# A Sinkhorn sort with a matrix column on each partition and row sums by fp32 matmul, and a stored order for every engine, in a fused attention and gating kernel

**Chip, cores, metric.** One core of a Trainium2 chip. The metric is device microseconds (us) of one execution, median over runs. Lower is better.

## The reference, cut to what matters

```python
P = sort_net                                   # (4, 8, 8, 8): 32 matrices of 8x8
for _ in range(5):
    P = exp(P - max(P, axis=-1))
    P = P / (sum(P, axis=-1) + 1e-9)           # rows
    P = P / (sum(P, axis=-2) + 1e-9)           # columns
k_sorted = einsum('bhij,bhjcd->bhicd', P, k_b) # 8 blocks of 96 rows are mixed
v_sorted = einsum('bhij,bhjcd->bhicd', P, v_b)
# attention inside each block of 96 rows, then x @ w_in, a scan over the
# 768 rows, silu gating, and @ w_out
```

The five iterations are tiny (2,048 numbers) but strictly serial, and nothing that needs sorted K or V can start before them.

## The kernel before

The program is a list of operations with dependences. A planner in the kernel orders them on the five engines when the program is built; what runs on the chip are five fixed lists, one for each engine, each run in order. The sort puts one 8x8 matrix on each of 32 partitions and takes seven steps an iteration, one on ScalarE (ACT) and six on VectorE (DVE):

```python
for it in range(5):
    op("sk_exp", ACT,  exp(E8, src))                     # 32x64
    op("sk_rs",  DVE,  tensor_reduce(RS, E9, add))       # row sums
    op("sk_rr",  DVE,  reciprocal(RS))
    op("sk_pa",  DVE,  tensor_tensor(PA8, E8, rs, mult))
    op("sk_cs",  DVE,  tensor_reduce(CS, PA9t, add))     # column sums
    op("sk_cr",  DVE,  reciprocal(CS))
    op("sk_pb",  DVE,  tensor_tensor(dst, PA8, cs, mult))
# ... cut: transpose on TensorE, copy, 8 small matmuls spread P over 128 partitions
op("lmat0", DVE, LALL = spread P * MASK)                 # block matrices of heads 0, 1
# warm-ups: matmuls with nothing to do, 48 in all
WARMS = (3, 3, 2, 2, 1)                                  # groups of 4 (last: 8)
# ... cut
op("vs%d_%d", PE, matmul(PS, LALL[head], VB[head]))      # sorted V of one head
op("vse%d_%d", ACT or DVE, copy to VSS)
op("vm%d", SP, 8 DMAs VA <- VSS)                         # "V move": re-lays a batch's V
P.schedule(8, pull=5.859375, stick=0.1, nudge=NUDGE)
```

(Schematic; names are the program's.) Sorted V of batches 1 to 3 needs eight value products, eight evictions to VSS and then the V move before its attention can begin.

The softmax here doesn't subtract the row's maximum and nothing guards it: scores larger than these inputs give would overflow.

## Time and profile before

| | kernel before |
|---|---|
| time | 123.95 us median of 3 runs (123.77 to 125.11) |
| profiled span | 121.7 us |
| TensorE (PE) busy | 92% of the span |
| LALL, the first sorted block matrices | starts at 12.26 us |
| a 128x128 matmul on PE takes 314 ns until, and 219 ns from | about 10.6 us |
| first V move leaves at | 28.55 us |

PE is the bound once sorted data are there (busy 103.75 of the 105.86 us from 12.74 to 118.6). Groups of the same matmuls in the timeline (columns: start us, us from the first start to the last end, engine, line, operation, operands, count, idle time before):

```profile
5.04 0.85 PE L609 MATMUL PSA<-IDENT,QB 128*64 128x128 bf16 x12 [0.92 <-DMA QB<-in_q_dram]
...
12.15 0.53 PE L609 MATMUL PSA<-IDENT,QB 128*64 128x128 bf16 x12
```

Twelve transposes of Q take 0.85 us at 5 us and 0.53 us at 12 us. I call PE *cold* and *warm* for these two rates; the warm-ups are meant to get from one to the other before LALL. The granted clock of the profile does not show the difference: it gives 1.00 for the first 12 us, but the trace's first clock record is at 10.86 us.

### The profile page before, as it was taken

To read this page: it belongs to the slowest core of one execution; us is meant where nothing else is said; L and a number is where in the kernel's file an instruction comes from. 1 tells how busy PE (TensorE), PEld (TensorE's weight loads), DVE (VectorE), ACT (ScalarE), POOL (GpSimd) and SP (SyncE) were. 2 spreads that over 40 slices of the span, in tenths; PEclk is the share of its full clock that TensorE was granted. 3 is DMA by queue.
4 is the path that set the end of the run, shared out by engine and by line. 5 is a ranking of instruction groups with operands and counts; after the bars stand their busy time and mean duration, and the time that the engine had idled before them with its cause. 6 is when DMAs were issued, how large, how long until landed. Compare 5 with 4: busy or idle time off the path is not lost.

```text
span 121.7 us, 3684 instructions
## 1 busy us (share of the span) xinstructions
PE 112.2 (92%) x1485; PEld 74.7 (61%) x1485; DVE 100.0 (82%) x239; ACT 84.0 (69%) x183; POOL 59.5 (49%) x84
## 2 busy tenths in 40 slices
PE   1689989999999999999999999999799999999990
PEld 1577778765766777667556586766466655554530
DVE  3774897999998999977599999999799999995300
ACT  4126879999868988898866977887634423365761
POOL 7999999999955620200028065000011396235500
PEclk9999999999999999999999999999999999999999
DMA  1999999999999999999999868289892000422665
GB/s 6 149 176 188 199 212 209 204 205 203 217 247 236 202 208 215 225 251 239 253 293 251 128 102 154 100 151 144 287 260 48 5 0 0 172 89 86 226 252 216
DMA packets 26305, 21.33 MB, mean 175 GB/s; under 512 B 7472, under 2 KB 22832, under 8 KB 26288
## 3 DMA queue, kind: packets, MB, share of 16 engines
q0 software_dynamic: 13824, 11.01, 58.3%
q1 hardware_dynamic: 12464, 10.08, 30.8%
q8 instruction: 12, 0.20, 0.6%
q14 instruction: 5, 0.04, 0.1%
HBM read 22.03 MB, written 6.29 MB: 233 GB/s over the span
## 4 chain that ended last, share of the span: by engine, by line
PE 66%; DMA 10%; DVE 9%; ACT 4%; SPq 4%; POOL 2%; issue 1%; POOLq 0%
PE PSA L800 31%; PE PSA L836 14%; DMA VA<-VSS 6%; PE PSA L733 5%; DVE XN L754 5%; DMA QB<-in_q_dram 4%; SPq L671 4%; PE PSA L703 4%; PE PSA L609 4%; PE PSA L625 3%; PE PSA L662 2%; ACT EX L713 2%; PE PSA L776 1%; DVE XT L417 1%; DVE RZ L745 1%
## 5 line engine op out<-in xcount | busy, mean ns | idle before, releaser
L819 POOL TENSOR_TENSOR GA<-GA,YS 128x384 bf16<-128x384 bf16 x30 | 27.2, 917 | 55.3 <-DVE GA L816 32.0
L800 PE MATMUL PSA<-XT,WIN 128*128 128x384 bf16 x256 | 45.4, 326 | 0.8 <-DVE XN L754 0.8
L800 PEld LDWEIGHTS PSA<-XT,WIN 128*128 128x128 bf16 x256 | 23.9, 98 | 16.3 <-DVE XN L754 0.9
L713 ACT ACTIVATE EX<-PSA 96x384 bf16<-96x384 f32 x64 | 26.3, 488 | 2.4 <-PE PSA L703 2.1
L813 ACT ACTIVATE TH<-PSA 128x384 f32<-128x384 f32 x32 | 15.7, 492 | 15.0 <-PE PSA L800 13.8
L836 PE MATMUL PSA<-WOUT,GA 128*128 128x512 bf16 (+1 forms) x100 | 23.2, 370 | 0.0
L754 DVE TENSOR_TENSOR XN<-PSA,RZ 96x320 bf16<-96x320 f32 (+2 forms) x49 | 21.7, 470 | 0.2
L816 DVE SCALAR_TENSOR_TENSOR GA<-TH,PSA 128x384 bf16<-128x384 f32 x32 | 17.0, 542 | 5.3 <-ACT TH L813 4.2
L415 ACT ACTIVATE OUTSB<-PSA 128x512 f32<-128x512 f32 (+1 forms) x23 | 13.4, 581 | 7.3 <-PE PSA L836 7.1
L807 DVE TENSOR_TENSOR_SCAN YS<-AEXP,YS,PSA 128x384 bf16<-128x384 f32 x16 | 15.7, 999 | 0.3 <-PE PSA L800 0.2
L807 DVE TENSOR_TENSOR_SCAN YS<-AEXP,PSA 128x384 bf16<-128x384 f32 x16 | 14.8, 940 | 0.7 <-PE PSA L800 0.7
L733 PE MATMUL PSA<-VA,EX 96*128 96x65 bf16 x256 | 13.7, 194 | 0.5 <-DVE XN L754 0.2
L836 PEld LDWEIGHTS PSA<-WOUT,GA 128*128 128x128 bf16 x100 | 9.0, 97 | 8.2 <-ACT OUTSB L415 0.3
L733 PEld LDWEIGHTS PSA<-VA,EX 96*128 96x128 bf16 x256 | 10.9, 98 | 4.7 <-DMA VA<-VSS 0.8
L745 DVE RECIPROCAL RZ<-PSA 96x5 f32<-96x5 f32 (+2 forms) x52 | 8.3, 175 | 2.0 <-PE PSA L733 1.6
L415 ACT ACTIVATE KTS<-PSA 128x768 bf16<-128x768 f32 x11 | 8.6, 811 | 1.4 <-PE PSA L625 1.3
L703 PE MATMUL PSA<-QTS,KTS 64*96 64x96 bf16 x256 | 9.5, 210 | 0.0
L703 PEld LDWEIGHTS PSA<-QTS,KTS 64*96 64x96 bf16 x256 | 7.2, 121 | 3.6 <-DVE KTS L417 0.4
L609 PE MATMUL PSA<-IDENT,QB 128*64 128x128 bf16 x192 | 7.8, 238 | 1.3 <-DMA QB<-in_q_dram 1.3
L415 ACT ACTIVATE VSS<-PSA 128x384 bf16<-128x384 f32 x19 | 8.4, 504 | 0.3 <-PE PSA L662 0.3
L625 PE MATMUL PSA<-LALL,KB 128*64 128x128 bf16 x192 | 7.4, 221 | 0.7 <-ACT EX L713 0.6
L427 POOL DMA_DIRECT2D QB<-in_q_dram x10 | 7.7, 782 | 0.3 <-issue 0.3
(60 smaller groups left out, 122.2 us busy)
## 6 DMA issues: line engine op xcount, KB each, us to landing
out_dram<-OUTSB SPq DMA_DIRECT2D x23, 256.0 KB, 2.5
VA<-VSS SPq DMA_DIRECT2D x24, 97.5 KB, 5.7
VB<-in_v_dram POOLq DMA_DIRECT2D x6, 384.0 KB, 20.1
KB<-in_k_dram POOLq DMA_DIRECT2D x6, 384.0 KB, 23.9
QB<-in_q_dram POOLq DMA_DIRECT2D x6, 384.0 KB, 21.5
WIN<-in_moe_w_in_dram POOLq DMA_DIRECT2D x1, 1024.0 KB, 11.1
QB<-in_q_dram POOLq DMA_DIRECT2D x4, 192.0 KB, 5.1
KB<-in_k_dram POOLq DMA_DIRECT2D x4, 192.0 KB, 6.1
```

The lines of the kernel that those rows point to most:

```text
L415: return eng.activation(dst, src, AF.Copy, scale=1.0 if scale is None else scale)
L609: ins = e.transpose(PSB[u.bank][64 * x:64 * x + 64, t * 128:(t + 1) * 128], QB[sl][:, 2 * pr + x, t * 64:(t + 1) * 64], IDENT[:, :])
L703: ins = e.matmul(PS[us[half, x].bank][0:BLK, il * BLK:(il + 1) * BLK], KTS[ks][r, i * BLK:(i + 1) * BLK], qt(r, i))
L713: op("ex%d_%d_%d" % (p, half, x), act_cost(HALF), lambda e, n, u=us[half, x], es=es, half=half: e.activation(EX[es][:, half, 0:HALF].rearr ...
L733: ins = e.matmul(PS[u.bank][:, (kk - k0) * 65:(kk - k0 + 1) * 65], EX[es][:, i // 4, (i % 4) * BLK:(i % 4) * BLK + 128], VA[vs][:, i, hx * ...
L754: return e.tensor_tensor(XN[xs][:, k0 * D:(k0 + nb) * D].rearrange("p (n d) -> p n d", d=D), pv(u, nb)[:, :, 0:64], bass.AP(RZ[rz], 0, [[6 ...
L800: ins = e.matmul(PS[u.bank][:, 0:HALF], WIN[:, c, col:col + 128], XT[(4 * b + c) % NXT][:, half * HALF:(half + 1) * HALF], start=(c == 0), ...
L807: op("sc%d_%d_%d" % (b, ch, half), {"DVE": 65 + 384 * 2.1}, lambda e, n, u=u: e.tensor_tensor_scan(YS[slot][:, :], AEXP[:, ch:ch + 1].to_b ...
L813: op("th%d_%d_%d" % (b, ch, half), act_cost(HALF), lambda e, n, u=w: e.activation(TH[ts][:, :], PS[u.bank][:, 0:HALF], AF.Tanh, scale=0.5) ...
L816: op("ga%d_%d_%d" % (b, ch, half), dve_cost(HALF), lambda e, n, u=w: e.scalar_tensor_tensor(GA[slot][:, :], TH[ts][:, :], 1.0, PS[u.bank][ ...
L819: op("um%d_%d_%d" % (b, ch, half), {"POOL": 900, "DVE": 500} if b == B - 1 and half else {"POOL": 900}, lambda e, n: e.tensor_tensor(GA[sl ...
L836: ins = e.matmul(PS[u.bank][:, 0:c1 - c0], GA[slots[ch]][:, tl * 128:(tl + 1) * 128], WOUT[:, ch, c0:c1], start=(ch == 0), stop=(ch == 3))
```

## The change

Intent: shorten the serial chain. A column of a matrix now lies on each partition (256 partitions in two halves of 128, which run interleaved). Sums over a matrix row then cross partitions and become an fp32 matmul with blocks of ones; column sums fall out of a multiply as its accumulated output; the column scaling is folded into the next exp as its per-partition scale. Four dependent steps and a matmul replace seven steps, and the ending is shorter. At the same time the planner's rule is replaced by a stored list for each engine.

```diff
-ORDER is worked out:  P.schedule(8, pull=5.859375, stick=0.1, nudge=NUDGE)
+ORDER is stored:      P.replay(8, ORDER)
-WARM = 7500.0        # planner: PE is warm from here, ns
+WARM = 6000.0
-WARMS = (3, 3, 2, 2, 1)          # 48 warm-up matmuls
+WARMS = (4, 2, 2, 2, 2, 2)       # 14 groups of 3
-op("ld_sort", SP, dma PIN <- sort_net)
+for x in range(2):
+    o1 = op("ld_sort%d" % x, SP, dma SX[x] <- 128 rows of 8)
+    if x: o1.deps[ld_s] = 1       # the second waits for the first
+  # first iteration: exp(SM <- SX, accum_out=SR), reciprocal, block product SB,
+  #   scaled copy SA, fp32 matmul SB x SA, reciprocal           (cut)
+  for it in range(1, 5):
+    op("sk_exp%d_%d", ACT, activation(SE, SA or PSUM, Exp, scale=SC))
+    op("sk_mm%d_%d",  PE,  matmul(acc, BO, SE))          # fp32, 128x8: row sums
+    op("sk_rr%d_%d",  DVE, reciprocal(rrow, acc))
+    op("sk_pa%d_%d",  DVE, scalar_tensor_tensor(SA, SE, 1.0, rrow, mult, mult, accum_out=SR))
+    op("sk_cr%d_%d",  DVE, reciprocal(SC, SR))
+  # one matmul per half in place of transpose, copy and 8 matmuls (cut)
```

All the rest of the program is the same work in another order.

## The prediction

> **What bounds the kernel now.** I read the page first, then the chain that ended last in order of time, then the table of stretches, then the timeline of the first 24 us. The page says that TensorE (PE) is the engine to look at:
>
> ```profile
> span 121.7 us, 3684 instructions
> PE 112.2 (92%) x1485; PEld 74.7 (61%) x1485; DVE 100.0 (82%) x239; ACT 84.0 (69%) x183; POOL 59.5 (49%) x84
> PE 66%; DMA 10%; DVE 9%; ACT 4%; SPq 4%; POOL 2%; issue 1%; POOLq 0%
> ```
>
> PE is busy for 92% of the span and carries 66% of the chain. The measured time, 123.95 us, is about 2.2 us longer than the profiled span. The table of stretches, cut where the first matmul on sorted data starts (12.74 us) and where PE ends (118.6 us), has columns busy us of PE, PEld, DVE, ACT, POOL, then granted clock, DMA share and GB/s:
>
> ```profile
> 12.74:15.00 2.26, 2.10 (x58) 1.69 (x60) 2.01 (x3) 2.26 (x4) 2.26 (x9) 1.00 1.31 201
> 15.00:18.00 3.00, 2.41 (x61) 2.05 (x57) 2.86 (x4) 2.57 (x7) 3.00 (x6) 1.00 1.22 213
> 18.00:24.00 6.00, 5.93 (x137) 4.97 (x132) 5.24 (x21) 5.64 (x12) 5.97 (x8) 1.00 1.20 206
> 24.00:60.00 36.00, 35.73 (x549) 24.15 (x549) 31.57 (x75) 31.79 (x76) 16.58 (x21) 1.00 1.27 224
> 60.00:118.60 58.60, 57.58 (x593) 34.74 (x590) 50.71 (x104) 36.31 (x77) 19.84 (x22) 1.00 0.61 146
> ```
>
> In these 105.86 us PE is busy 103.75: only 2.1 us of idle time are left. So the time is (start of sorted work, 12.74) + (about 104 us of PE work) + (2 us of idle) + (tail of 3.1 us after PE's end: one eviction of 0.60 and a store of 2.5). The sort iteration can change the first term only. The timeline shows it as a chain of single small instructions, one after the other on ScalarE (ACT) and VectorE (DVE):
>
> ```profile
> 1.09 1.28 ACT L517 ACT_TABLE_LOAD   x1 [1.09 <-DVE PSA L492]
> 2.39 0.22 ACT L517 ACTIVATE PSA<-PIN 32x64 f32<-32x64 f32 x1
> ...
> 4.09 0.22 ACT L517 ACTIVATE PSA<-PBT 32x64 f32<-32x64 f32 x1 [1.49 <-DVE PBT L529]
> 4.34 0.22 DVE L520 TENSOR_REDUCE RS<-PSA 32x8 f32<-32x72 f32 x1 [0.28 <-ACT PSA L517]
> 4.60 0.19 DVE L522 RECIPROCAL RS<-RS 32x8 f32<-32x8 f32 x1
> ...
> 11.38 0.20 PE L545 MATMUL PSA<-IDENT,PBF 32*64 32x32 bf16 x1
> 11.62 0.18 DVE L548 CAST PT<-PSA 64x32 bf16<-64x32 f32 x1 [0.73 <-PE PSA L545]
> ...
> 12.26 1.42 DVE L560 TENSOR_TENSOR LALL<-PSA,MASK 128x256 bf16<-128x256 f32 x2 [0.46 <-PE PSA L554]
> ```
>
> The reader is to see three things. Exp to exp is 4.09 - 2.39 = 1.70 us: seven steps of about 0.243 us. The table load was over (2.37) just as the input landed (0.75 + 1.6 = 2.35), so it cost nothing. And after the fifth iteration a transpose, a copy and eight matmuls stand before LALL, the block matrices, at 12.26.
>
> [...]
>
> **The change part by part.** The 256 matrix rows go to two halves of 128 partitions, which run interleaved.
>
> Start. The first exp now also needs a constant that GpSimd (POOL) writes, and in POOL's new list that memset stands behind iota, the first Q load and another memset. In the trace POOL's first load is issued from 1.35 to 2.24, so the constant is there at about 2.4. In the old program the table load waited for the memsets of DVE (1.09, just after the second one ended at 1.01) and the exp alone for the DMA; I expect the same of the new one. Then the table load runs from about 2.45 to 3.75, and the first exp starts at 3.75 in place of 2.39: **+1.35 us** on the path.
>
> First iteration: [...]reciprocal 0.2; [...]reciprocal 0.2. About 1.9 us, so the second exp is at 5.65.
>
> Iterations two to five: [...]matmul to the next DVE instruction: 0.24 is what the bf16 one at 11.38 took[...]; reciprocal 0.22; [...]reciprocal 0.19. Sum 1.51 against 1.70. The other half's three DVE operations fit between, since independent DVE operations follow each other at less than their duration (two 96x4 reciprocals took 0.24 together). I take 1.55. The fifth exp is at 5.65 + 3 x 1.55 = 10.3.
>
> End: [...]reciprocal, multiply, mask reduction beside it, reciprocal: 1.0, masked product 128x128 0.3, matmul 0.25. LALL starts at 10.3 + 2.4 = **12.7 against 12.26**. So the shorter iteration (4 x 0.15 = 0.6) and the shorter ending (three steps gone, about 0.5) are eaten by the late table load. Without that the start would be 11.4.
>
> After LALL. I counted PE's new list: the order of all work is new. Changes of tile mode go from 55 to 59[...], seven groups of three warm-up matmuls come after LALL's matmul[...], and both first evictions (V and K) are on ACT one after the other, where before one was on DVE beside it; the first attention exp may come 1 us later than 15.16. The last seven output pieces are alike, so the tail stays. Against this: the order is a stored list, not the outcome of a rule, and I suppose that it was chosen because it was short; it can win at most the 2.1 us of idle time[...]. I put -1.3 there. Sum: +0.4 (start) + 0.4 (head and modes) - 1.3 = -0.5, so **123.4 us**.
>
> **The rivals.** (a) The sort path really becomes shorter: if the table load is hidden as before, or fp32 matmuls take 0.4, LALL comes at 10.8 to 11.4 and all of PE's work moves forward by about 1 to 1.5; with a better order 121.3. For it: the design aims at this. Against: the old trace puts the table load behind the memset wait, and K and V data limit it: the fourth to twelfth loads land about 1 us apart, from 8.95 to 17.6 (10.35 + 7.3), whatever the sort does, and the first K load is now the seventh, about 11.7. (b) The lockstep of two halves is slow: DVE, ACT and PE each run in order, so each half waits for the other; with 1.75 per iteration and a PE clock that warms late, LALL comes at 13.6 and the time is 125. For it: the old PE needed until about 10.6 to warm with 48 dense warm-ups, the new ones are sparser. (c) The start is hidden anyway and only the new order counts: POOL now has products of the gating before some loads, so late loads could make PE wait at 40 to 70 us; or the order closes PE's idle time. 122 to 125.
>
> **Range and chances.** (a) has some 25%, (b) 25%, the middle the rest. 2% is 2.5 us; faster than 121.5 needs both an earlier start and a better order: 14%. Slower than 126.4 needs (b) and a worse order: 6%. Range 121.2 to 125.4; the old runs alone spread from 123.77 to 125.11.
>
> **What would show it.** In the new profile: the table load starting after 2.3 and the first exp near 3.7 (if at 2.4, rival a); exp to exp 1.5 to 1.6 for one half (1.75 or more, rival b); matmul to reciprocal 0.5 to 0.6; LALL at 12.0 to 13.4; PE's idle time from there to its end 1 to 2.5 us. I am wrong if LALL starts before 11.5 or PE's work after it, idle included, differs by over 2 us from 105.9.

The sums were made with the cut terms. The first iteration's 1.9 us is 0.4 for the two reciprocals and 1.5 of cut terms. The 1.51 of an iteration is 0.41 for its two reciprocals (0.22 and 0.19 are durations of DVE steps in the profile above) and 1.10 of cut terms for exp, matmul and multiply (the 0.24 that still stands beside the matmul is a measured time and not the term); the range for "matmul to reciprocal" rests on them too. The 2.4 of the ending is 1.55 for the steps that still stand and about 0.85 of cut terms. The 1.55 is an estimate from the trace of the kernel before: 0.19 + 0.22 + 0.38 + 0.19 for the four small steps, about 0.3 for 128 columns from the 0.43 and 0.96 us that masked products of 256 and 768 columns took, and 0.24 for the matmul. The "0.4 (head and modes)" was for four more changes of tile mode; that a change costs time was not shown. With all of this the forecast came to +0.4 + 0.4 - 1.3 = -0.5, so 123.4 us. (One 96x4 reciprocal alone took 0.17 us, beside the 0.24 for two.)

## The result and the profile after

| | before | after |
|---|---|---|
| time, median | 123.86 us (123.75 to 125.11, 4 runs) | **135.69 us** (135.12 to 137.80, 4 runs) |
| ratio of fast runs | 1 | 1.0915 (95%: 1.0815 to 1.1015) |
| profiled span, clock | 121.7 us, 1.00 | 133.2 us, 0.974 |

A ratio here and below is the mean time of one kernel's fast runs over the mean of the other's fast runs of the same rounds, so it is not quite the ratio of the medians that stand beside it. A run is called slow when it lies over 1.5% above the fastest run of its kernel; the others are fast.

The page of the changed kernel:

```profile
span 133.2 us, 3729 instructions
...
PE 120.4 (90%) x1496; PEld 80.9 (61%) x1496; DVE 98.1 (74%) x251; ACT 87.3 (66%) x201; POOL 58.8 (44%) x90
...
PEclk9999999999999995599999999999999999999999
```

PE is busy 120.4 us in place of 112.2 for the same real work, and the clock row (tenths, 40 slices) falls to half near 52 us. So some of PE's time went into running slowly and some into waiting. The first 16 us, ACT and the first LALL on DVE:

```profile
2.51 1.28 ACT L494 ACT_TABLE_LOAD   x1 [2.51 <-POOL SX L488]
3.80 0.21 ACT L494 ACTIVATE SM<-SX 128x9 f32<-128x9 f32 x1
3.92 0.19 ACT L494 ACTIVATION_READ_ACCUMULATOR SM<-SX 128x1 f32 x1
...
5.32 0.21 ACT L494 ACTIVATE SM<-SX 128x9 f32<-128x9 f32 x1 [0.68 <-PE PSA L508]
...
5.53 0.26 ACT L519 ACTIVATE SE<-PSA,SC 128x8 f32<-128x8 f32 x1
...
7.47 0.29 ACT L519 ACTIVATE SE<-SA,SC 128x8 f32<-128x8 f32 x1
9.00 0.65 ACT L519 ACTIVATE SE<-SA,SC 128x8 f32<-128x8 f32 x2 [1.24 <-DVE SC L532]
11.30 0.65 ACT L519 ACTIVATE SE<-SA,SC 128x8 f32<-128x8 f32 x2 [1.66 <-DVE SC L532]
...
15.37 0.42 DVE L556 TENSOR_TENSOR LALL<-PSA,MASK 128x256 bf16<-128x256 f32 x1
```

The first half's exps are at 5.53 and 7.47: 1.94 us apart. The pairs at 9.00 and 11.30 hold both halves, 2.3 apart. The old exps were 1.70 apart. LALL comes 3.1 us later than before. On PE:

```profile
16.49 0.85 PE L630 MATMUL PSA<-LALL,KB 128*64 128x128 bf16 x12
...
46.25 0.81 PE L805 MATMUL PSA<-XT,WIN 128*128 128x384 bf16 x4
46.90 0.33 PE L667 MATMUL PSA<-VB,LALL 128*128 128x384 bf16 x1
50.60 0.49 PE L738 MATMUL PSA<-VA,EX 96*128 96x65 bf16 x6 [3.38 <-DMA VA<-VSS]
...
51.85 1.49 PE L805 MATMUL PSA<-XT,WIN 128*128 128x384 bf16 x4
```

Three things are to be seen. At 16.49 PE is still cold (0.85 for twelve, 0.53 before), although its list has been without a gap from 4.69 to 15.65; it turns warm near 18.9, against 10.6. After the matmul of 46.90 it stops for 3.38 us, from 47.22 on, for a V move. Behind that stop four projections take 1.49 us instead of 0.81. The same stretch in the table by stretches (busy us of PE, PEld, DVE, ACT, POOL; granted clock; DMA share; GB/s):

```profile
48.00:52.00 4.00, 1.40 (x10) 0.92 (x11) 1.44 (x3) 0.55 (x2) 0.00 (x0) 0.71 1.30 212
52.00:56.00 4.00, 4.00 (x23) 2.15 (x22) 2.28 (x7) 2.18 (x6) 1.72 (x2) 0.50 1.29 199
```

In the kernel before:

```profile
48.00:52.00 4.00, 4.00 (x65) 2.65 (x63) 3.76 (x9) 3.37 (x8) 0.91 (x1) 1.00 1.28 235
52.00:56.00 4.00, 4.00 (x86) 3.00 (x84) 3.10 (x9) 3.51 (x8) 0.00 (x0) 1.00 1.21 250
```

It has 65 and 86 matmuls in these two windows, at clock 1.00. Now there are 10 and 23. The trace's own clock records say the same: half clock is granted from 49.71 us, 2.5 us into the stop, for 6.83 us. At a granted clock of 0.50 that is up to 3.4 us of PE work lost (an estimate, half of 6.83), as much as the stop itself. The V move was late mainly because it left late. From the queue of the DMA issues, before and then after:

```profile
28.55 5.22 SPq L671 DMA_DIRECT2D VA<-VSS  x8
```

```profile
37.06 30.53 SPq L676 DMA_DIRECT2D VA<-VSS  x16
```

(The second line joins two moves: the first leaves at 37.06.) Its last piece landed at 50.5, against 40.3 before: 8.5 of these 10.2 us are the later start. It left late because the last value evictions of that batch stand on ACT behind 20 small normalisations (XN) and two activations of the gating (TH), with ACT busy 11.98 of the 12 us from 24 to 36 us:

```profile
34.14 1.76 ACT L756 ACTIVATE XN<-PSA,RZ 96x64 bf16<-96x64 f32 x8
35.72 0.56 ACT L818 ACTIVATE TH<-PSA 128x384 f32<-128x384 f32 x1
36.09 0.94 ACT L373 ACTIVATE VSS<-PSA 128x384 bf16<-128x384 f32 x2
```

So there were two suspects: the new sort, with its cold PE, and the stored order. All runs below gave a result that agrees with the reference, those with rounding to bf16 included.

### The profile page after: what moved, and what is told of

The parts are those of the page before. It is cut to its first block, busy times and chain, and to the rows that moved or that the text cites. A ratio compares the mean times of both kernels' runs of the same rounds, so it can differ in the third digit from the quotient of the medians.

```text
span 133.2 us, 3729 instructions
## 1 busy us (share of the span) xinstructions
PE 120.4 (90%) x1496; PEld 80.9 (61%) x1496; DVE 98.1 (74%) x251; ACT 87.3 (66%) x201; POOL 58.8 (44%) x90
## 4 chain that ended last, share of the span: by engine, by line
PE 66%; ACT 13%; DMA 9%; SPq 7%; issue 1%; POOL 1%; DVE 1%; POOLq 0%; ACTq 0%
PE PSA L805 27%; PE PSA L841 14%; DMA VA<-VSS 9%; SPq L676 7%; PE PSA L738 4%; PE PSA L630 4%; ACT EX L718 4%; PE PSA L708 3%; PE PSA L548 3%; PE PSA L614 3%; ACT XN L756 3%; PE PSA L524 2%; ACT VSS L373 2%; PE PSA L667 2%; PE PSA L652 1%
## 5 line engine op out<-in xcount | busy, mean ns | idle before, releaser
L805 PE MATMUL PSA<-XT,WIN 128*128 128x384 bf16 x256 | 49.1, 335 | 0.4 <-ACT XN L756 0.3
L718 ACT ACTIVATE EX<-PSA 96x384 bf16<-96x384 f32 x64 | 26.9, 490 | 2.6 <-PE PSA L708 2.4
L373 ACT ACTIVATE OUTSB<-PSA 128x512 f32<-128x512 f32 x19 | 11.2, 597 | 8.5 <-PE PSA L841 7.4
L738 PEld LDWEIGHTS PSA<-VA,EX 96*128 96x128 bf16 x256 | 11.7, 100 | 8.4 <-issue 4.1
L812 DVE TENSOR_TENSOR_SCAN YS<-AEXP,PSA 128x384 bf16<-128x384 f32 x16 | 14.9, 939 | 1.4 <-PE PSA L805 1.4
L373 ACT ACTIVATE VSS<-PSA 128x384 bf16<-128x384 f32 x22 | 10.3, 508 | 5.4 <-PE PSA L667 5.3
L373 ACT ACTIVATE KTS<-PSA 128x768 bf16<-128x768 f32 x12 | 9.5, 825 | 0.8 <-PE PSA L630 0.8
L614 PE MATMUL PSA<-IDENT,QB 128*64 128x128 bf16 x192 | 8.3, 243 | 0.0
L556 POOL TENSOR_TENSOR LALL<-PEXP,MASK 128x512 bf16<-128x512 bf16 x6 | 6.4, 1059 | 3.5 <-ACT PEXP L571 3.5
## 6 DMA issues: line engine op xcount, KB each, us to landing
WIN<-in_moe_w_in_dram POOLq DMA_DIRECT2D x1, 1024.0 KB, 14.9
```

The source lines that it names most:

```text
L373: return eng.activation(dst, src, AF.Copy, scale=1.0 if scale is None else scale)
L614: ins = e.transpose(PSB[u.bank][64 * x:64 * x + 64, t * 128:(t + 1) * 128], QB[sl][:, 2 * pr + x, t * 64:(t + 1) * 64], IDENT[:, :])
L718: op("ex%d_%d_%d" % (p, half, x), act_cost(HALF), lambda e, n, u=us[half, x], es=es, half=half: e.activation(EX[es][:, half, 0:HALF].rearr ...
L738: ins = e.matmul(PS[u.bank][:, (kk - k0) * 65:(kk - k0 + 1) * 65], EX[es][:, i // 4, (i % 4) * BLK:(i % 4) * BLK + 128], VA[vs][:, i, hx * ...
L805: ins = e.matmul(PS[u.bank][:, 0:HALF], WIN[:, c, col:col + 128], XT[(4 * b + c) % NXT][:, half * HALF:(half + 1) * HALF], start=(c == 0), ...
L812: op("sc%d_%d_%d" % (b, ch, half), {"DVE": 65 + 384 * 2.1}, lambda e, n, u=u: e.tensor_tensor_scan(YS[slot][:, :], AEXP[:, ch:ch + 1].to_b ...
```

## Experiments

### Which part of the change costs? (n1, n2)

n1 keeps the new sort and puts everything else back into the old order (the warm-up groups that stood behind LALL are left out). n2 keeps the old sort and takes the new order for everything else.

```diff
 n1 = kernel after
-WARMS = (4, 2, 2, 2, 2, 2)
+WARMS = (4, 2, 1, 0, 0, 0)
-ORDER = stored new lists
+ORDER = new sort's head + the old kernel's own lists from there on

 n2 = kernel before
-P.schedule(...)
+P.replay(8, old sort's head + new stored lists from there on)
```

> New sort, everything else in the old order of each engine. Theory 1 (the late sort is the cause: LALL at 15.37 in place of 12.26, and the work behind it is thrown out of step): 129 to 134 us, most of the loss of 11.8 stays. Theory 2 (the new stored order of the rest is the cause): the sort costs only its own delay of about 3 us, so 126 to 128 us, and the V moves of the second batch start near 31.5 (28.5 + 3) and not near 37.

> Old sort, everything else in the new stored order. Theory 1: LALL near 12.3 again and 123 to 126 us. Theory 2: LALL near 12.3, but PE still idles before the V moves of the second batch have landed and the time is 129 to 134 us.

| | time (median) | ratio to before | LALL | first V move |
|---|---|---|---|---|
| n1, new sort, old order | 128.22 us | 1.0392 (1.0301 to 1.0484) | 14.86 | 31.52 |
| n2, old sort, new order | 131.95 us | 1.0675 (1.0596 to 1.0755) | 11.83 | 33.27 |

Both parts cost, and the order costs more. Their sum, 10.7%, agrees with the whole (9.15%, interval 8.15 to 10.15) about as well as the intervals allow, so there is no large interaction. n1's time lies just above the 126 to 128 us of its theory 2, with the V move where that theory has it; n2 is inside the range of its theory 2. In n2 the old sort even has LALL earlier than in the kernel before, and PE is warm by about 8.4 us; what it waits for comes later:

```profile
PE PSA L682 <- DMA VA<-VSS: 3.3, 1, 3.3
...
PE PSA L611 <- DMA VB<-in_v_dram: 1.9, 1, 1.9
```

(engine and line waited for: us in total, times, longest). The first of these stops, for VB, starts at 42.4 us; the one for a V move at 62.5, so it is that of the batch after the one that stopped the changed kernel. In the kernel before the wait for V moves is 0.2 us in all, and there is none for VB.

### The late start of the sort (n3, n5)

The prediction gave the late table load 1.35 us of the path. n3 takes it away with a dummy exp ahead of everything on ACT. n5 does that too and lets the second half's input load go out at once.

```diff
 n3
+act.activation(DUM, const 0.0, Exp)      # first on ACT
 n5 = n3 and
+ld_sort1.deps.clear()                    # does not wait for ld_sort0's landing
```

> The changed kernel with one dummy exp in front on ScalarE, which waits for nothing, so that the table load is over before the sort input lands. First exp at 2.4 to 2.5 in place of 3.80. If the table load delays the sort one for one, LALL comes at 14.0 to 14.2 and the time falls by 1.3 us or somewhat more: 133 to 134.5. If PE is what the sort waits for in the head, LALL gains less than 0.7 and the time stays within 0.7 of 135.5.

> The changed kernel with two edits at its start: the table load comes first on ScalarE, and the second sort input no longer waits for the first one's landing. Theory 'head': the late start was held by the table load AND the second input, so moving one alone gave nothing; with both moved exp0_1 starts at 4.0 to 4.4 us (5.53 before the edit), LALL at 13.7 to 14.2 (15.37), and the time falls by 1.2 to 2.0 us, to 133.7 to 134.5. Rival: iterations stretch because the TensorE is cold anyway; LALL stays above 15 and the time within 0.5 us of the changed kernel.

n3: 136.59 us (135.23 to 138.07), no ratio could be given; its two fast runs, 135.23 and 135.37, are level with the changed kernel's 135.12 to 136.07. LALL came at 15.15 (15.37). n5: 135.89 us median of 4, two of them near 134.4 and fast, two near 137.6 and slow; ratio of the fast runs 1.0817 (1.0768 to 1.0865). LALL at 14.09, in the profile of a slow run. The line of n3 that explains it:

```profile
2.52 0.21 ACT L495 ACTIVATE SM<-SX 128x9 f32<-128x9 f32 x1 [0.28 <-POOL EPSR L463]
...
5.32 0.21 ACT L495 ACTIVATE SM<-SX 128x9 f32<-128x9 f32 x1 [1.96 <-DMA SX<-in_sort_net_dram]
```

The first exp moved from 3.80 to 2.52, but the second half's first exp stayed at 5.32, waiting for its input, and ACT's list has it ahead of the first half's second exp, which stayed at 5.53. In the changed kernel the table load covered that wait. Two causes of the late start lay side by side; only taking both away moved the chain, by 1.28 us, and the fast runs lie about one point lower (1.0915 to 1.0817, in different rounds). The theory 'head' holds for LALL; the intervals of the two ratios overlap, so the gain in time is not shown.

### Warm-ups and the cold PE (n4, n7, n10, n11)

n4 takes all 14 groups of warm-ups out of the changed kernel. n7 is the new sort with the first half always first, both early starts of n5, three groups of warm-ups, and the old order of the rest. n11 is n7 with 14 groups that fill the gaps of the sort on PE (and one constant matmul, sk_eps1, a place earlier); n10 is n11 with the exponentials (SE) and the block of ones (BO) in bf16; the trace lists a row-sum matmul once there (0.19 to 0.21 us while PE is cold) and twice in fp32 (0.54 to 0.59 us for the pair in n11).

```diff
 n4
-14 groups warm*  (removed from PE's list)
 n7 = new sort, old order of the rest, n5's two edits
-PE:  sk_mm0_1 sk_mm1_0 ... sk_mm1_2 sk_mm0_3     halves in lockstep
+PE:  sk_mm0_2 sk_mm1_1 ... sk_mm0_3 sk_mm1_2     half 0 first
+WARMS = (3, 0, 0, 0, 0, 0)
 n11 = n7 and
+WARMS = (14, 0, 0, 0, 0, 0), one to three groups in each gap before LALL
 n10 = n11 and
-BO, SE: F32
+BO, SE: BF16
```

> The changed kernel without the 14 groups of three warm-up matmuls, all else as it was. If PE's list is what makes the sort slow (fp32 matmuls behind warm-ups on a PE that is busy without a break from 4.7 to 15.2 us), the 21 or so warm-ups before LALL give back up to 2 us there and LALL comes at 13.5 to 14.5. If the clock matters more, PE warms later still and the time stays at 135 or rises.

> The new sort with the old order of all the rest, both sort inputs and the table load early, the first half of the sort always given priority and the halves in antiphase, three warm-up groups. If the sort's loss (3.4 to 4.4 us against the kernel before) is mainly start and mutual waiting of the two halves: LALL of the first half at 10.8 to 11.8 (12.26 in the kernel before, 14.86 in the new sort with the old order), time 122.5 to 125. Rival: an iteration of the new sort has at least 1.75 us of latency with TensorE cold, whoever goes first; LALL 13 to 14, time 126 to 128.

> As n7 (new sort, first half first, old order of the rest), but the exponentials and the block of ones are bf16[...], and 14 groups of warm-up matmuls fill the gaps. n7 had LALL at 11.81, before the 12.26 of the kernel before, and still lost 3.5 us: its TensorE stayed slow until 21.9 us (10.6 in the kernel before). Theory 'cold TensorE': here the 128-column matmuls take 219 ns instead of 314 from 9 to 13 us on, LALL at 11.0 to 12.0, time 121.5 to 124. Rival: a slow TensorE costs nothing there because data limit the phase; time stays at 127 to 128. The rounding to bf16 may fail the comparison; the time counts all the same.

> As n10 but fp32 as in the change. If fp32 matmuls of 8 columns keep the TensorE from warming (they hold it for some 0.5 us[...]), it is fast only after 15 us or later, LALL at 12.3 to 13.5, time 125.5 to 128. If the missing warm-ups of n7 alone were the reason, the same as n10.

| | ratio to before | time (median) | LALL | PE warm near | first transposes of XN | span |
|---|---|---|---|---|---|---|
| before | 1 | 123.9 us | 12.26 | 10.6 | 20.15 | 121.7 |
| n1 | 1.0392 | 128.22 us | 14.86 | 17.2 | 23.08 | 126.1 |
| n7 | 1.0285 (1.0224 to 1.0345) | 127.98 us | 11.81 | 21.9 | 24.50 | 126.5 |
| n11 | 1.0156 (1.0099 to 1.0213) | 125.99 us | 13.20 | 14.9 | 22.87 | 123.5 |
| n10 | 1.0095 (1.0047 to 1.0143) | 125.17 us | 11.84 | 14.5 | 21.90 | 123.4 |

(The clock records put the change to full clock at 10.86, 17.48, 22.20, 15.09 and 14.46 us for these five; the table's values, read from matmul durations, lie up to 0.3 lower.)

n4, in the changed kernel's order, took 132.26 us, ratio 1.0676 (1.0564 to 1.0789): **better** without warm-ups than with them. Its LALL was at 14.03 and its PE warm near 18.8, just as with them. So the 14 groups of the change bought no warmth; they stood in front of the sort's own matmuls. (In the changed kernel the exps at 9.00 fed a matmul that began only at 9.99, behind three warm-ups and twelve transposes.) The gain of 2.4 points need not come from the head alone. In the profiles, with LALL 1.34 us earlier, the V move left 1.24 us earlier, PE waited 2.3 us for V moves and not 4.1, and the half clock behind the stop lasted 3.41 us and not 6.83. The seven groups behind LALL are gone from PE too. n4 is level with n2 (1.0675), which has the old sort.

n7 is the telling one. Its LALL (11.81) came as its expectation had it, its time (122.5 to 125 expected) did not. LALL is 0.45 us *earlier* than in the kernel before, which was the whole intent of the change, and it still lost 2.85%. PE at the same work in n7:

```profile
16.66 0.85 PE L614 MATMUL PSA<-IDENT,QB 128*64 128x128 bf16 x12
...
24.50 0.34 PE L781 MATMUL PSA<-IDENT,XN 96*128 96x96 bf16 x4
```

and in n10:

```profile
15.48 0.53 PE L615 MATMUL PSA<-IDENT,QB 128*64 128x128 bf16 x12
...
21.90 0.34 PE L782 MATMUL PSA<-IDENT,XN 96*128 96x96 bf16 x4
```

In n7 PE ran the first ten microseconds after LALL cold, and reached the first normalised output 4.35 us after the kernel before (24.50 against 20.15), nearly the whole of its loss in span (4.8). Apart from that one constant matmul, n11 differs from n7 in warm-ups on PE alone (the lists of the other four engines are the same): LALL came 1.4 us *later*, and yet the time fell by 1.3 points, because PE was warm at 14.9. That is the cold PE shown by itself: warmth was worth more than 1.4 us of LALL. My guess that fp32 matmuls as such keep PE from warming was wrong: n10 and n11 warm within 0.6 us of each other (one profile each). The fp32 form costs latency instead (LALL 13.20 against 11.84), and 0.6 points of the time, whose intervals just overlap. n10 has LALL where n7 has it, was warm 7.4 us sooner, and got back 1.9 of n7's 2.85 points (with bf16 in it too). It missed its expectation all the same: PE warm by 13 us and at most 124 us.

What makes PE warm is not settled: the changed kernel's list was without a gap from 4.69 to 15.65 and it needed until 18.9; n11, with other fillers in the same sort, was warm at 14.9 and n7 at 21.9.

### The late V moves (n6, n8, n9)

n6 moves the last four value products of the second batch, and their evictions, to directly behind the first of their group. n8 also moves two value products of the third batch up, and the loads of the third and fourth batch ahead of the gating products on GpSimd (POOL). n9 makes n8's repair in n2, with the old sort.

```diff
 n6
 PE :  ... vs1_1 + [vs1_2 vs1_0 vs1_6 vs1_4] ...          (from further down)
 ACT:  ... vse1_1 + [vse1_0 vse1_6 vse1_4] xn0_8 xn1_12 ...
 DVE:  ... rz0_8 + [vse1_2] ...
 n8 = n6 and
 PE :  ... vs2_6 + [vs2_0 vs2_7] ... ;  ACT: ... vse2_5 + [vse2_0 vse2_7] ...
 POOL: ... lmat28 + [all later loads, lmat24] um0_2_0 ...
 n9 = n2 with the same moves
```

> The changed kernel with one edit to the stored order: the last four value products of the second batch and their evictions come directly behind the first of their group on TensorE, ScalarE and VectorE, ahead of the group of normalisations. Theory 'late V moves': in the stored order these evictions are the last ones on ScalarE (near 36 us), the V moves leave at 37 instead of 28.5, TensorE idles 3.4 us and then runs at a lower clock. Then the V moves leave at 30 to 33 us, the wait of 3.4 us and the fall of the granted clock after 48 us are gone, and the time is 129 to 131 (4.5 to 6.5 less). Rival (the order's cost lies in the total of ScalarE work in 24 to 36, or in the later output part): the V moves leave earlier, but the time falls by less than 2 us.

> The changed kernel with the order mended in both places where V data came late: the value products of the second batch first (as in n6), the last two of the third batch moved up too, and the loads of the third and fourth batch ahead of the gating products on GpSimd. After n6 the wait had only moved to the next batch (2.4 us at 66, then half clock). Theory 'late V moves': both waits of over 2 us and both falls of the clock are gone, granted clock 1.0 in the profile, time 128.5 to 130.5. Rival (the stored order loses on many small places): time stays at 131.5 or more although no long wait is left; or the early loads collide with the V moves and a wait returns.

> The old sort with the stored new order mended in the same two places. n2 (same without the mending) was 1.0675 of the kernel before. Theory 'late V moves': most of the 6.75% goes, ratio 1.00 to 1.025, no V wait over 1 us, clock 1.0. Rival: ratio stays above 1.04.

| | ratio to before | time (median) | first V move | longest wait of PE for a V move |
|---|---|---|---|---|
| after | 1.0915 | 135.69 us | 37.06 | 3.4 us |
| n6 | 1.0661 (1.0601 to 1.0721) | 132.79 us | 32.71 | 2.4 us, at 66 |
| n8 | 1.0597 (1.0543 to 1.0651) | 131.39 us | 33.54 | none listed |
| n2 | 1.0675 | 131.95 us | 33.27 | 3.3 us, at 62.5 |
| n9 | 1.0282 (1.0224 to 1.0339) | 127.67 us | 27.90 | none listed |

In n6 the stop at 47 us is gone, but its profile shows it again one batch later:

```profile
64.00:68.00 4.00, 1.98 (x39) 1.26 (x37) 2.08 (x5) 3.14 (x7) 0.00 (x0) 0.97 1.04 260
68.00:72.00 4.00, 3.58 (x25) 2.22 (x26) 2.63 (x7) 0.86 (x2) 0.00 (x0) 0.50 0.02 6
```

Repairing one batch let PE run into the next one. n6 missed its expectation of 131 us at most. Its two slow runs have mean clocks of 0.972 and 0.987, its three fast ones 1.000: the second stop costs the clock only in some executions, and the ratio 1.0661 is of runs without that cost. n8 and n9 have neither the long waits nor the fall of the clock behind them (1.00 in every stretch up to 110 us). They gained 3.2 points with the new sort (1.0915 to 1.0597) and 3.9 with the old one (1.0675 to 1.0282), in different rounds. So late V moves and late V loads, with the half clock behind them, are somewhat more than half of what the order costs (3.9 of 6.75 points with the old sort). The loads by themselves are not shown to matter: from n6 to n8 the intervals overlap. n9's expectation (at most 1.025) was just missed, n8's (130.5 us at most) by 0.9 us. What remains, 2.8% in n9, has no single place. The spans differ by 3.1 us (124.8 against 121.7); PE is busy 1.1 us more, and of the 2.0 us of added idle time nearly all lies in 12 to 48 us:

```profile
24.00:36.00 12.00, 10.52 (x144) 7.02 (x143) 9.18 (x27) 10.79 (x38) 10.93 (x14) 1.00 1.27 216
```

PE is idle 1.48 us here, 0.27 in the kernel before, and likewise 0.4 us more in each neighbour. Which edges of the list cause these small waits I did not settle. One suspicion, argued and not tested: the planner's constant says that PE is warm from 6.0 us (7.5 before), while the trace of the changed kernel shows 18.9; a list made under that supposition expects PE's work earlier than it comes.

n8 against n9 is a second reading of the sort's cost: 1.0597 against 1.0282, 3.1 points, beside the 3.9 of n1. The changed kernel against n2 gives 2.4, and n4 against n2 nothing. So the sort has no one price: it depends on the warm-ups and on which stops the order leaves behind it.

### A try for a version that beats both (n12)

```diff
 n12 = n10 and
+two groups of warm-ups ahead of everything on PE; ONESR, EPSR in BF16
+second half's iteration 3 ahead of the larger LALL product, its last matmul ahead of vt1
```

> A try for a version that beats the kernel before. As n10 (1.0095, LALL at 11.84, TensorE fast from 14.5 us) with two groups of warm-ups ahead of everything on TensorE, the two initial constant matmuls in bf16 too, and the last two iterations of the second half pulled ahead of the second part of LALL and of the V products, since in n10 TensorE waited 0.8 us for the second half's last product at 17. If warming earlier is what is left: TensorE fast by 11 to 13 us, LALL at 11.3 to 11.9, ratio 0.98 to 1.0. If the second half only takes DVE's time from LALL, or the clock's switch stays at 14.5: ratio 1.005 to 1.015.

126.43 us, ratio 1.0127 (1.0071 to 1.0182): no better than n10, and in the range that the expectation gave to the rivals, though for a reason that none of them named. The head did what was wanted, LALL at 11.04 and PE warm by 10.9. Then:

```profile
15.05 0.85 PE L631 MATMUL PSA<-LALL,KB 128*64 128x128 bf16 x12 [1.45 <-DMA KB<-in_k_dram]
```

PE stopped 1.45 us for the next K load and was cold again until about 21 us (0.85 for twelve; the profile is of a slow run with a mean clock of 0.973, the fast ones have 0.986 to 1.000, so I take from it where PE waits, not how long). Half clock was granted 0.85 us into this stop, with 0.46 us of idle time shortly before; in the changed kernel it came 2.5 us into the stop of 3.38. The kernel before reached the same point of its list at 14.29 without that wait. That K load landed at 13.95 there and at 14.91 here, so part of the wait is the later landing; but with either, a sort that ends before 12 us runs into K's arrival (an estimate: the kernel before was there 2.03 us after its LALL, so the landing at 13.95 answers to a LALL at 11.92). No version beat the kernel before; n10 is within 2% of it.

## Why the prediction was wrong, point by point

- **"At most the 2.1 us of idle time" and "I put -1.3 there."** This is the step that failed most. I counted what a good list could win and not what a bad one could lose, and "chosen because it was short" was a supposition. The term is about +8 us, not -1.3 (n2: 131.95 against 123.7, medians of the fast runs). Somewhat more than half of it is late V data with the half clock behind it (n9). Rival (c) named a neighbouring place, loads late behind gating products at 40 to 70 us, and its direction was right; but I gave it 125 us at the most. One look in the new lists at where the last eviction before each V move stands would have shown the risk.
- **"I take 1.55" and LALL at "12.7 against 12.26".** Wrong: about 2.0 between exps, and 15.37. The 1.51 was a sum of latencies of one half alone. It left out that PE runs its list in order: the fp32 matmul stood behind the other half's matmul, warm-ups and transposes of Q (from 9.00 to 9.99 in the case shown above). The single durations were close: matmul start to reciprocal 0.57 us at 6.10 and 0.63 at 7.63, exp with scale 0.26 to 0.30 (without a scale it took 0.21), multiply with accumulator 0.17 + 0.08; together 1.08 to 1.18, against 1.10 in the terms that are cut. Rival (b), lockstep with 1.75 or more, was right, with LALL later than its 13.6.
- **Table load and first exp "from about 2.45 to 3.75".** Right (2.51 to 3.80). But its +1.35 was not on the path alone: beside it lay a second wait that I did not read, the second input behind the first (n3, n5).
- **"Seven groups of three warm-up matmuls come after LALL's matmul".** Named, but left out of the sum: its +0.4 for "head and modes" is no more than the figure for the mode changes. In the trace PE is busy with these 21 matmuls for 2.69 us between 15 and 27 us. Their point, that PE must be warm at LALL, was only mentioned in rival (b). In n7 the cold PE is the larger part of the new sort's loss.
- **"K and V data limit it".** Right, as n12's wait of 1.45 us shows: even the intended gain had little room. (The first K load is the sixth in POOL's new list and not the seventh; it landed at 12.15, against "about 11.7".)
- **"The tail stays" and the 0.4 for "head and modes".** The tail, from PE's end on, grew from 3.1 to 3.5 us. The changes of mode are 59 as counted; no run measures what one costs.
- **Range and chances.** 6% for slower by over 2% came from asking for both (b) and a worse order, as if both were rare. Both came true, and either alone was enough: n1 is at 128.22 and n2 at 131.95.

The checks that I set did their work: LALL was to be at 12.0 to 13.4 (15.37), and PE's work after the first sorted matmul, idle time included, within 2 us of 105.9. It runs from 15.85 to 129.73, which is 113.9.

## What to carry to other kernels

A change that replaces an ordering rule by a stored list is two changes: measure the list with the old code, and for each long transfer look where the last of its inputs stands in its engine's list. When a serial chain is moved onto TensorE, look at what stands in front of it in that engine's list: here exps at 9.00 fed a matmul that began at 9.99. Look at the filler matmuls too: with three groups of them (n7) TensorE was cold until 21.9 us, with 14 in the gaps (n11) until 14.9, and LALL 0.45 us earlier with a cold TensorE (n7) lost 2.85%. Two waits that lie side by side hide each other: taking the table load away moved LALL by 0.22 us (n3), taking both waits away by 1.28 (n5), so seeing no gain from one does not show that it cost nothing.
